# Output quarters eight slots behind instead of sixteen, reordered first loads and early attention, whole GpSimd masks, mx written over hp

## The chip, the cores and the metric

One core of a Trainium2 chip, one launch. The metric is the device time in microseconds (us). PE stands for TensorE's matmuls, PEld for its weight loads, DVE for VectorE, ACT for ScalarE, POOL for GpSimd. The profiler's span is some 1.7 us shorter than the time of the same execution (336.13 us timed, 334.4 us profiled, for the kernel before).

## The reference, cut to what matters

```python
# q, k, v: batch 8, heads 8, sequence 576, head size 64
scores = q @ k.T / 8
mask   = abs(pos_i - pos_j) <= 32            # sliding window
attn   = softmax(where(mask, scores, -1e9)) @ v
x      = attn as [4608 tokens, 512]
h      = x @ w_in                             # [4608, 2048]
g      = h if h >= 1; 0 if h <= -1; else (h + 1)**2 / 4
out    = g @ w_out                            # [4608, 512], float32
```

## The kernel before

The MLP is cut into 144 **slots**: 18 tiles of 256 tokens by 8 column chunks. Each slot runs 8 matmuls into `hp` and turns `hp` into a piece of `gT`. A slot's length is the time from its first hp matmul to that of the next slot, counted from the trace's records. Attention is woven in at fixed slots: `scores` (matmuls, Exp on ACT, then a multiplication by a 0/1 mask), `sums` (matmuls with `pt`, the masked exponentials, then the division, which gives `xT`), and transposes of q and k. The activation uses g = min(r, 1) * max(h, r) with r = relu(h/2 + 1/2).

```python
LAG = 16
for a in range(NF * NB + LAG):               # 144 slots + 16
    t, f = divmod(a, NF)
    eng = None if a < 14 else V if a < 28 else P       # who multiplies by the mask
    ...
        hp = ps_h.tile([128, 2, TB], FP, name="hp", tag="hp")     # PSUM, two buffers
        ... 8 matmuls xT, w_in -> hp ...
        rr = ewp.tile([128, 2, TB], FP, name="rr")                # SBUF
        A.activation(rr, hp, AF.Relu, scale=0.5, bias=0.5)
        mx = ewp.tile([128, 2, TB], FP, name="mx")                # SBUF
        V.tensor_max(mx, hp, rr)
        V.scalar_tensor_tensor(gT[t][...], rr, 1.0, mx, op0=ALU.min, op1=ALU.mult)
    ... attention events of this slot ...
    if a >= LAG:
        ... 4 matmuls gT, w_out -> op: the output of slot a - 16 ...

def mask(eng, p, m):
    if eng is P:                              # GpSimd: four pieces of 256 columns
        for h in range(2):
            for i in range(p.shape[2]):
                P.tensor_mul(p[:, h, i], p[:, h, i], m[:, h, i])
    elif eng is not None:
        eng.tensor_mul(p, p, m)
```

All loads of the start but the first q are issued by GpSimd in one sequence: most of w_in in pieces of 256 columns, then the rest of batch 0's q and k mixed with w_in, then batch 1, and w_out near the end.

The softmax here doesn't subtract the row's maximum and nothing guards it: scores larger than these inputs give would overflow.

## Time and profile before

| | before |
|---|---|
| time, median of the first 3 runs (range) | 337.27 us (335.68 to 337.89) |
| profiled span, granted TensorE clock | 334.4 us, 0.985 |
| PE busy | 310.2 us, 93% of the span |
| DVE, ACT, POOL busy | 236.2, 194.6, 160.9 us |
| PE idle up to 14.9 / to 52 / to 88 / to 315 / to the end | 1.2 / 10.4 / 2.9 / 5.7 / 4.0 us |

The last row is each stretch's length less its PE busy time, from the first table quoted in the prediction. The 93% hides what matters. Only 24 us of idle PE exist, 10 of them in one early stretch, and the last 15 us of busy PE are work that stands alone at the end only because it was postponed. With the PE's work unchanged, this kernel can get faster in two ways: less idle time of PE, or no PE work left over for a time when nothing else runs.

The view of waits of the kernel before (engine, line, what it waited for; us in total, number of times, longest), cut to the sums that wait for a GpSimd mask:

```profile
PE bb L294 <- POOL pt L201: 5.3, 7, 1.3
```

### The profile page before, as it was taken

What the parts mean: (1) busy time and instruction counts of PE and PEld (TensorE: products, weight loads), DVE (VectorE), ACT (ScalarE), POOL (GpSimd) and SP (SyncE); (2) the same over time, 40 slices, a digit from 0 to 9 for tenths busy, and PEclk for the clock granted to TensorE, in tenths of its full rate; (3) what the DMA queues carried; (4) which work ended last, traced back from release to release, by engine and by line L of the source; (5) the groups of instructions that cost most, each with busy time, mean ns of one, the idle gap of its engine ahead of it and who ended that gap; (6) DMA issues with size and microseconds to landing.
All of it is one profiled execution on the core that took longest, in us unless ns stands there. A gap on an engine that the chain in (4) does not pass through costs nothing.

```text
span 334.4 us, 8639 instructions
## 1 busy us (share of the span) xinstructions
PE 310.2 (93%) x3647; PEld 203.9 (61%) x3647; DVE 236.2 (71%) x355; ACT 194.6 (58%) x320; POOL 160.9 (48%) x236
## 2 busy tenths in 40 slices
PE   8957798979999989998999999997999999999995
PEld 3535575556666656665666666664666666666642
DVE  2343888778788777886788877885788877878800
ACT  3635894766765746565656656664675666544411
POOL 8986647950155973577524953297343334000000
PEclk9976999999999999999999999999999999999999
DMA  9999999999079997699440999179941100000021
GB/s 145 133 170 151 153 159 165 162 148 79 33 163 107 87 128 157 81 89 159 104 102 33 149 129 179 61 48 166 135 105 55 44 31 34 33 31 33 31 94 63
DMA packets 122118, 34.53 MB, mean 103 GB/s; under 512 B 108768, under 2 KB 117216, under 8 KB 122080
## 3 DMA queue, kind: packets, MB, share of 16 engines
q0 software_dynamic: 93216, 18.06, 71.1%
q1 hardware_dynamic: 28864, 15.93, 18.9%
q8 instruction: 28, 0.46, 0.6%
q14 instruction: 10, 0.08, 0.1%
HBM read 36.70 MB, written 9.44 MB: 138 GB/s over the span
## 4 chain that ended last, share of the span: by engine, by line
PE 53%; POOL 23%; issue 9%; ACT 6%; DVE 4%; DMA 3%; POOLq 0%; ACTq 0%
PE op L455 24%; PE hp L433 22%; POOL pt L201 10%; POOL vn L101 5%; PE bb L294 4%; POOL kn L93 3%; POOL qn L93 2%; ACT pt L236 2%; DMA kn<-in_k_dram 2%; DMA w_in<-in_moe_w_in_dram 2%; PE tp L184 1%; PE bb L228 1%; POOL w_in L105 1%; POOL kn L85 1%; DVE mx L439 1%
## 5 line engine op out<-in xcount | busy, mean ns | idle before, releaser
L433 PE MATMUL hp<-xT,w_in 128*128 128x256 bf16 x1152 | 151.0, 275 | 3.4 <-DVE xT L306 1.9
L455 PE MATMUL op<-w_out,gT 128*128 128x512 bf16 x576 | 145.6, 380 | 0.0
L433 PEld LDWEIGHTS <-w_in 128*128 128x128 bf16 x1152 | 111.9, 98 | 45.3 <-issue 4.7
L437 ACT ACTIVATE rr<-hp 128x512 f32<-128x512 f32 x144 | 85.8, 596 | 88.6 <-PE hp L433 82.5
L439 DVE TENSOR_TENSOR mx<-hp,rr 128x512 f32<-128x512 f32 x144 | 99.2, 689 | 37.7 <-ACT rr L437 36.7
L201 POOL TENSOR_TENSOR pt<-pt,mask 128x256 bf16<-128x256 bf16 (+1 forms) x112 | 72.2, 675 | 108.0 <-ACT pt L236 85.6
L440 DVE SCALAR_TENSOR_TENSOR gT<-rr,mx 128x512 bf16<-128x512 f32 x144 | 105.4, 732 | 4.9
L455 PEld LDWEIGHTS <-gT 128*128 128x128 bf16 x576 | 53.4, 98 | 42.8
L306 DVE TENSOR_TENSOR xT<-bb,rc 128x512 bf16<-128x512 f32 (+1 forms) x32 | 21.1, 658 | 29.4 <-ACT rc L301 29.4
L236 ACT ACTIVATE pt<-bb 128x1024 bf16<-128x1024 f32 (+1 forms) x33 | 33.2, 1011 | 12.8 <-PE bb L228 11.8
L459 ACT COPY osb<-op 128x512 f32<-128x512 f32 x36 | 21.0, 583 | 17.5 <-PE op L455 17.1
L294 PE MATMUL bb<-pt,ones 64*64 64x256 bf16 (+3 forms) x352 | 21.2, 256 | 9.2 <-POOL pt L201 5.3
L101 POOL DMA_DIRECT2D vn<-in_v_dram x32 | 27.7, 890 | 0.0
L301 ACT ACTIVATE rc<-lr 128x512 f32<-128x512 f32 (+2 forms) x40 | 23.5, 589 | 1.3
L294 PEld LDWEIGHTS <-ones 64*64 64x64 bf16 x352 | 11.7, 105 | 19.0 <-issue 15.6
L300 ACT ACTIVATE lr<-bb 128x512 f32<-128x512 f32 (+2 forms) x40 | 22.0, 550 | 0.7 <-PE bb L294 0.6
L294 PE MATMUL bb<-pt,vn 64*64 64x128 bf16 (+3 forms) x712 | 19.4, 204 | 0.0
L85 POOL DMA_DIRECT2D kn<-in_k_dram x24 | 13.0, 547 | 13.0 <-DMA w_out<-in_moe_w_out_dram 6.2
L294 PEld LDWEIGHTS <-vn 64*64 64x64 bf16 x712 | 17.0, 107 | 0.0
L228 PE MATMUL bb<-qT,kT 64*64 64x128 bf16 x520 | 13.5, 217 | 0.9 <-DVE kT L187 0.8
L93 POOL DMA_DIRECT2D qn<-in_q_dram x10 | 12.4, 1250 | 0.2 <-issue 0.2
L93 POOL DMA_DIRECT2D kn<-in_k_dram x10 | 12.3, 1238 | 0.0
(45 smaller groups left out, 105.9 us busy)
## 6 DMA issues: line engine op xcount, KB each, us to landing
out_dram<-osb SPq DMA_DIRECT2D x36, 256.0 KB, 2.1
vn<-in_v_dram POOLq DMA_DIRECT2D x32, 144.0 KB, 7.8
qn<-in_q_dram POOLq DMA_DIRECT2D x10, 288.0 KB, 6.2
kn<-in_k_dram POOLq DMA_DIRECT2D x10, 288.0 KB, 8.5
w_out<-in_moe_w_out_dram POOLq DMA_DIRECT2D x4, 512.0 KB, 8.5
kn<-in_k_dram POOLq DMA_DIRECT2D x24, 72.0 KB, 4.0
w_in<-in_moe_w_in_dram POOLq DMA_DIRECT2D x12, 128.0 KB, 5.0
qn<-in_q_dram POOLq DMA_DIRECT2D x20, 72.0 KB, 6.7
```

The costliest lines, as they stand in the source:

```text
L93: nc.gpsimd.dma_start(out=x[:, :, h], in_=src[b, NY * h:NY * h + NY].rearrange("y s d -> (y s) d") .rearrange("(u p) d -> p u d", p=128))
L101: nc.gpsimd.dma_start(out=vn[b][64 * a:64 * a + 64, :, h], in_=v[b, y:y + 2].rearrange("y s d -> (y s) d") .rearrange("(c r) d -> r c d", ...
L201: P.tensor_mul(p[:, h, i], p[:, h, i], m[:, h, i])
L236: A.activation(p, ps[:, :, :128 * n].rearrange(like, y=m), AF.Exp, scale=D ** -0.5)
L294: nc.tensor.matmul(bb[HD[h], a, o + c0:o + c1], ones[HD[a]] if c is None else vn[b][HD[a], c, h], p(a, h), start=n == 0, stop=True, skip_g ...
L300: A.activation(lr[:, :, :D0], bb[:, :, D0:2 * D0], AF.Ln)
L301: A.activation(rc[:, :, :D0], lr[:, :, :D0], AF.Exp, scale=-1.0)
L433: nc.tensor.matmul(hp[:, j], w_in[:, kk, 256 * f + 128 * j:256 * f + 128 * j + 128], xT[:, kk, r0:r0 + TB], start=n == 0, stop=n == 3)
L437: A.activation(rr, hp, AF.Relu, scale=0.5, bias=0.5)
L439: V.tensor_max(mx, hp, rr)
L440: V.scalar_tensor_tensor(gT[t][:, 2 * f:2 * f + 2], rr, 1.0, mx, op0=ALU.min, op1=ALU.mult)
L455: nc.tensor.matmul(op, gT[tt // 2][:, ff, 128 * (tt % 2):128 * (tt % 2) + 128], w_out[:, ff], start=ff == 0, stop=ff == 2 * NF - 1)
```

## The change

The intent: put part of the output matmuls into the waits of the start so that they don't stand at the end; bring what the start waits for sooner; shorten the GpSimd masks; and, with mx written over hp, take away the stretching of GpSimd's mask pieces and DVE's gT where they overlap (before, up to 1192 and 1148 ns, against medians of 668 and 692). The diff, cut to its core:

```diff
-    [w_in in eight pieces of 256 columns, then batch 0's rest mixed with w_in, then batch 1, v, w_out 0 to 3]
+    w = [(load_w_in, c, c + d, h) for c, d in ((0, 256), (256, 256), (512, 512), (1024, 512), (1536, 512)) for h in range(2)]
+    x = halves(0, 1)                                   # rest of batch 0's q (4 loads) and k (4)
+    put(w[:4] + x[:4] + w[4:5] + x[4:] + w[5:])
+    mix(halves(1, 0), [(load_w_out, 0)])
+    put([(load_w_out, 1), (load_w_out, 2)] + [(load_v, 1, n) for n in range(4)])
+    mix(halves(1, 1), [(load_w_out, 3)])
...
     def mask(eng, p, m):
-        if eng is P:
-            [four pieces]
-        elif eng is not None:
+        if eng is not None:
             eng.tensor_mul(p, p, m)
...
-    LAG = 16
+    PEM = 28
+    quarters = {11: ([], [0]), 12: ([], [1]), 13: ([], [2]), 14: ([], [4, 5]), 15: ([6], [3, 7])}
...
-    at(4, scores ...)  at(5, ...)  at(6, ...)  at(13, sums)  at(14, sums)
+    at(2, scores ...)  at(3, ...)  at(4, ...)  at(5, ...)  at(15, sums, sums)
-    for n, a in enumerate((12, 13, 20, 21, 22, 26, 27)):
+    for n, a in enumerate((11, 12, 19, 20, 22, 26, 27)):
         at(a, seq[n][1])
...
-    for a in range(NF * NB + LAG):
+    for a in range(NF * NB + NF):
...
-        eng = None if a < 14 else V if a < 28 else P
+        eng = None if a < 12 else V if a < PEM else P
+        pre, post = quarters.get(a, ([], [a - NF] if a >= 2 * NF else []))
...
-            mx = ewp.tile([128, 2, TB], FP, name="mx")
+            mx = ewp.tile([128, 2, TB], FP, name="mx") if a < PEM else hp
```

A **quarter** is four output matmuls. Four quarters make one 128-token output. Not shown in this cut: the transposes of the rest of batch 0's q and k move from slots 2 and 3 to slot 1, and two early slots instead of six take their hp from the output's PSUM buffers.

More of the change, by code (lines that the diff above doesn't have):

```diff
@@ L134 @@
         V.memset(t[:, 0:PAD], 0.0)
-    for c in range(0, 1024, 256):
-        for h in range(2):
-            load_w_in(c, c + 256, h)
     def mix(small, large):
@@ L146, in halves, with put @@
         return [(load_long, b, half, t, y) for t in range(2) for y in range(NY)]
-    mix(halves(0, 1), [(load_w_in, 1024, 1280, h) for h in range(2)] + [(load_w_in, 1280, 1536, h) for h in range(2)])
-    for h in range(2):
-        load_w_in(1536, 2048, h)
-    mix(halves(1, 0), [(load_v, 1, 0), (load_v, 1, 1)])
-    load_v(1, 2)
-    load_v(1, 3)
-    load_w_out(0)
-    load_w_out(1)
-    mix(halves(1, 1), [(load_w_out, 2)])
-    load_w_out(3)
+    def put(todo):
+        for fn, *x in todo:
+            fn(*x)
+    w = [(load_w_in, c, c + d, h) for c, d in ((0, 256), (256, 256), (512, 512), (1024, 512), (1536, 512)) for h in range(2)]
[4 more added lines that the diff above has]
+    mix(halves(1, 1), [(load_w_out, 3)])
     mix(halves(2, 0), [(load_v, 2, n) for n in range(4)])
-    for fn, *x in halves(2, 1):
-        fn(*x)
+    put(halves(2, 1))
     kT = {}
@@ L196, in mask @@
     def mask(eng, p, m):
-        if eng is P:
-            for h in range(2):
-                for i in range(p.shape[2]):
-                    P.tensor_mul(p[:, h, i], p[:, h, i], m[:, h, i])
-        elif eng is not None:
+        if eng is not None:
             eng.tensor_mul(p, p, m)
@@ L385, in steps @@
         yield (sums, b, 0, MAIN, S), (scores8, b)
-    at(4, (scores, 0, (0, 1), (0, 2), (2, 4)), (scores8, 0, ps_o))
-    at(5, (sums, 0, 0, TB, MAIN), (scores, 0, (1, 2), (0, 2), (2, 4)))
-    at(6, (sums, 0, 1, TB, MAIN, ps_s), (sums, 0, 0, MAIN, S))
+    at(2, (scores, 0, (0, 1), (0, 2), (2, 4)), (scores8, 0, ps_o))
+    at(3, (sums, 0, 0, TB, MAIN), (scores, 0, (1, 2), (0, 2), (2, 4)))
+    at(4, (sums, 0, 1, TB, MAIN, ps_s))
+    at(5, (sums, 0, 0, MAIN, S))
     seq = [x for b in range(1, B) for x in steps(b, 224)]
-    at(13, seq[0][0])
-    at(14, (*seq[1][0], ps_s))
-    for n, a in enumerate((21, 22, 23, 27)):
+    at(15, seq[0][0], (*seq[1][0], ps_s))
+    for n, a in enumerate((20, 22, 23, 27)):
         at(a, seq[2 + n][0])
-    for n, a in enumerate((12, 13, 20, 21, 22, 26, 27)):
+    for n, a in enumerate((11, 12, 19, 20, 22, 26, 27)):
         at(a, seq[n][1])
@@ L400 @@
         at(a, seq[6 + n][0], seq[7 + n][1] if n < len(sl) - 1 else None)
-    for b, half, *a in ((0, 1, 2, 3), (1, 0, 9, 11), (1, 1, 18, 19), (2, 0, 24, 25), (2, 1, 28, 29)):
+    for b, half, *a in ((0, 1, 1, 1.5), (1, 0, 9, 10), (1, 1, 17, 18), (2, 0, 24, 25), (2, 1, 28, 29)):
         for t in range(2):
@@ L410, with quarter @@
             xps.setdefault(a + 9 + 2 * t, []).append((b, t))
-    gT = {}
-    for a in range(NF * NB + LAG):
+    gT, op = {}, {}
+    def quarter(x):
+        tt, ff = divmod(x, 4)
+        if tt not in op:
+            op[tt] = ps_o.tile([128, DM], FP, name="op", tag="op"), []
+        o, done = op[tt]
+        for j in range(4 * ff, 4 * ff + 4):
+            nc.tensor.matmul(o, gT[tt // 2][:, j, 128 * (tt % 2):128 * (tt % 2) + 128], w_out[:, j],
+                             start=not done, stop=len(done) == 2 * NF - 1, skip_group_check=True)
+            done.append(j)
+        if len(done) == 2 * NF:
+            osb = osp.tile([128, DM], FP, name="osb")
+            A.copy(osb, o)
+            nc.sync.dma_start(out=out[128 * tt:128 * tt + 128, :], in_=osb)
+    for a in range(NF * NB + NF):
         t, f = divmod(a, NF)
-        eng = None if a < 14 else V if a < 28 else P
+        eng = None if a < 12 else V if a < PEM else P
+        pre, post = quarters.get(a, ([], [a - NF] if a >= 2 * NF else []))
         for b, x in loads.get(a, []):
@@ L426 @@
             r0 = TB * t % RING
-            if a < LAG and a % 4 > 1 and not 3 < a < 8:
+            if a in (6, 7):
                 hp = ps_o.tile([128, 2, TB], FP, name="hp", tag="op")
@@ L437 @@
             A.activation(rr, hp, AF.Relu, scale=0.5, bias=0.5)
-            mx = ewp.tile([128, 2, TB], FP, name="mx")
+            mx = ewp.tile([128, 2, TB], FP, name="mx") if a < PEM else hp
             V.tensor_max(mx, hp, rr)
             V.scalar_tensor_tensor(gT[t][:, 2 * f:2 * f + 2], rr, 1.0, mx, op0=ALU.min, op1=ALU.mult)
+        for x in pre:
+            quarter(x)
         ends = []
@@ L449 @@
             end()
-        if a >= LAG:
-            for x in range(4 * (a - LAG), 4 * (a - LAG) + 4):
-                tt, ff = divmod(x, 2 * NF)
-                if ff == 0:
-                    op = ps_o.tile([128, DM], FP, name="op", tag="op")
-                nc.tensor.matmul(op, gT[tt // 2][:, ff, 128 * (tt % 2):128 * (tt % 2) + 128], w_out[:, ff],
-                                 start=ff == 0, stop=ff == 2 * NF - 1)
-                if ff == 2 * NF - 1:
-                    osb = osp.tile([128, DM], FP, name="osb")
-                    A.copy(osb, op)
-                    nc.sync.dma_start(out=out[128 * tt:128 * tt + 128, :], in_=osb)
-        if a in tps:
-            copies = [tpose(b, n, t, (A.copy, V.tensor_copy)[i if a > LAG else 0], tp1((ps_s, ps_n)[i]))
-                      for i, (b, n, t) in enumerate(tps[a])]
+        for x in post:
+            quarter(x)
+        for part in (a, a + 0.5):
+            copies = [tpose(b, n, t, (A.copy, V.tensor_copy)[i if a > 15 else 0], tp1((ps_s, ps_n)[i]))
+                      for i, (b, n, t) in enumerate(tps.get(part, []))]
             for x in copies:
```

## The prediction

> **What bounds the kernel now.** I read the busy time of each engine by stretch first, because shares of the whole span mix stages. The columns after the stretch are its length, then busy us of PE, PEld, DVE, ACT and POOL, the granted TensorE clock, and the DMA's share and rate.
>
> ```profile
> 0.00:14.90 14.90, 13.71 (x168) 6.88 (x169) 4.26 (x18) 8.17 (x11) 13.16 (x28) 1.00 1.26 138
> 14.90:52.00 37.10, 26.66 (x427) 19.64 (x426) 23.32 (x37) 23.59 (x40) 25.82 (x43) 0.86 1.22 160
> 52.00:88.00 36.00, 33.11 (x457) 21.79 (x457) 28.56 (x45) 22.68 (x36) 16.84 (x23) 1.00 1.56 126
> 88.00:315.00 227.00, 221.35 (x2527) 148.63 (x2526) 177.62 (x256) 136.63 (x228) 105.11 (x144) 1.00 0.79 91
> 315.00:334.40 19.40, 15.36 (x75) 7.01 (x72) 2.44 (x4) 3.53 (x6) 0.00 (x0) 1.00 0.18 68
> ```
>
> Up to 52 us the PE waits for loads and for the first attention batch: 10.4 us idle, at a mean clock of 0.86. From 88 to 315 us the PE is the bound (5.7 us idle). From 315 us on only the PE works. The PE's timeline shows the tail, and the pace of a slot (one pass of the main loop: 8 hp matmuls, and from slot 16 on 4 op matmuls):
>
> ```profile
> 312.91 1.04 PE L433 MATMUL hp<-xT,w_in 128*128 128x256 bf16 x8
> 313.79 1.03 PE L455 MATMUL op<-w_out,gT 128*128 128x512 bf16 x4
> 314.65 1.04 PE L433 MATMUL hp<-xT,w_in 128*128 128x256 bf16 x8
> 315.52 14.84 PE L455 MATMUL op<-w_out,gT 128*128 128x512 bf16 x68
> ```
>
> Starts differ by 0.87 us, so a slot without attention costs 1.74 us of PE, and four op matmuls 0.87. The last line is the price of a lag of 16 slots: 64 of these 68 matmuls were owed from the start, when w_out had not come.
>
> The start, in the same view:
>
> ```profile
> 21.81 1.17 PE L184 MATMUL tp<-ident,qn 128*64 128x128 bf16 x18 [3.17 <-DMA qn<-in_q_dram]
> 27.14 1.17 PE L184 MATMUL tp<-ident,kn 128*64 128x128 bf16 x18 [2.34 <-DMA kn<-in_k_dram]
> 38.46 1.91 PE L433 MATMUL hp<-xT,w_in 128*128 128x256 bf16 x16 [1.08 <-DVE xT L309]
> 52.09 0.82 PE L433 MATMUL hp<-xT,w_in 128*128 128x256 bf16 x6 [1.48 <-DVE xT L306]
> ```
>
> The rest of batch 0's q and k, queued behind and between w_in, stops PE twice; the last line is inside slot 16, which so starts in effect at about 51.7 us (52.09 less two matmuls already done).
>
> In the steady stretch four slots (45, 62, 81, 99) are longer than their matmuls need, by 1.7, 1.7, 0.7 and 2.4 us as PE's matmul starts show: 6.5 us, all in front of sums that wait for a GpSimd mask. The POOL timeline before the last of them:
>
> ```profile
> 217.82 2.69 POOL L201 TENSOR_TENSOR pt<-pt,mask 128x256 bf16<-128x256 bf16 x4 [6.43 <-ACT pt L236]
> 220.46 2.50 POOL L93 DMA_DIRECT2D qn<-in_q_dram  x2
> 222.95 2.44 POOL L93 DMA_DIRECT2D kn<-in_k_dram  x2
> 225.35 3.44 POOL L101 DMA_DIRECT2D vn<-in_v_dram  x4
> 228.73 3.56 POOL L201 TENSOR_TENSOR pt<-pt,mask 128x256 bf16<-128x256 bf16 x4
> ```
>
> Mask, loads and mask form one chain of 14.5 us on POOL. The second mask takes 3.56 us where others take 2.5, and the two lines' own views (ns min/median/max) say why:
>
> ```profile
> L201 POOL TENSOR_TENSOR pt<-pt,mask x112: 361/668/1192, 91.0 to 284.2; 128x256 bf16<-128x256 bf16 x88, 128x96 bf16<-128x96 bf16 x24
> L440 DVE SCALAR_TENSOR_TENSOR gT<-rr,mx x144: 691/692/1148, 17.7 to 317.1; 128x512 bf16<-128x512 f32 x144
> ```
>
> Both have a tail of about 1.15 us, and in the timeline these long ones overlap each other.
>
> [...] gT (rr and mx, both SBUF) stretches from 692 to 1148 ns, while mx (one PSUM input) never exceeds 693. [...] In this trace undisturbed starts are 0.625 us apart at 256 columns and 0.32 at 96, so 1.9 ns per column and 0.14 us fixed[...]. [...] matmuls between 20.3 and 30.5 us start 213 ns apart instead of 108, after PE stood from 18.6 to 21.8.
>
> **Part by part.**
>
> *Tail.* The output runs 8 slots behind instead of 16. Eight quarters of four op matmuls move ahead of slot 16: 8 x 0.87 = **-6.9 us** at the end, where nothing lies beside them. Total PE work is unchanged, so this is gained only if the early stretch takes these 6.9 us in its waits: the question is when slot 16 starts.
>
> *Loads and early stretch.* In the before trace POOL's issues wait for the transfer eight issues earlier, which dates landings: the first w_in piece at 14.3 us, the eighth at 19.1, so 896 KB in 4.8 us or 186 KB/us. The new order is 512 KB w_in, 288 qn, 256 w_in, 288 kn, 256 w_in, then 1024 w_in. At that rate qn lands at 17.7 us (21.8 before), kn at 20.6 (27.1), the third w_in piece near 22. Pure w_in of 512 columns ran slower (110 KB/us of written bytes by my count of the trace's packets around 24.5 us), so I place the end of w_in at 29 to 30 us, the next q and k at 34 to 35.5, and, scaling the mean of 151 KB/us that the old order kept to 52 us, w_out 1 and 2 at 38 and 41, v of batch 1 at 45, w_out 3 at 47.5.
> PE from slot 2 (about 22.5): I add slot by slot the matmul work that the old trace shows (hp 0.87, 18 transposes 0.72, scores with their mask 0.9, two sums 1.3, quarter 0.87): slots 2-5 6.5, 6-8 2.6, 9-10 3.2, 11-14 9.4, 15 4.7: 26.4 us. The clock should be halved in part again (PE idles from 17 to 22 here too): +2.3 us of it. Slot 16 would come at 51.2, but needs xT from the sums in slot 15; before, xT came 3 us after such sums, which makes 52 to 53. Against 51.7: **+1 us**. So I expect no earlier slot 16, only eight quarters done for free in the old waits.
>
> *Masks 20 to 30.* Scores are a slot further ahead of their sums in the one place (slot 22) where sums waited 1.3 us for a DVE mask: **-1.2 us**.
>
> *Whole GpSimd masks, mx in PSUM.* One mask of 1024 columns: 0.14 + 1024 x 1.9 ns = 2.1 us, against 2.5 undisturbed. With mx written over hp, gT has one SBUF input, so the extra 1.0 us of a disturbed mask goes too. In the chain above the first mask gives 0.5 and the second 1.4 us back, of a wait of 2.4; the other three waits (1.7, 1.7, 0.7) are below such a gain and vanish. **-6.0 us** (6.5 less 0.5 left).
>
> *Price of mx in PSUM.* hp is now freed by gT, 0.73 us later. In plain slots of the old trace gT ends 0.35 us (0.30 at the end) before the next hp into that buffer starts, so nothing stalls. In 17 slots it ends later than, or within 60 ns of, that start, 3.8 us in sum; without the stretched gT about 1.3 us remains: **+1.3 us**.
>
> Sum: 337.3 - 6.9 + 1.0 - 1.2 - 6.0 + 1.3 = 325.5 us.
>
> **Rivals.** (a) *The start takes the tail's gain.* If w_in in 64-partition pieces keeps 110 KB/us, or the halved clock lasts to 30.5 us, slot 16 slips 2 to 4 us: 328 to 330. For: the 10 us at half clock, and PE has 6.9 us more to do before slot 16. Against: qn and kn come 4 and 6 us sooner. (b) *hp's release becomes the bound.* If a PSUM destination, or reading and writing one bank at once, makes mx or gT over 0.3 us longer, each of 116 slots stalls: 0.1 us beyond the slack is 12 us, giving 337 or worse. Against: PSUM sources cost nothing visible (xT and mx 692 ns, like gT); an in-place PSUM write occurs nowhere in this trace. (c) *The start gains too.* If DMA keeps 186 KB/us and the clock stays up, slot 16 starts 3 to 4 us sooner: 321. (d) *A whole mask is not cheaper*, or its four-dimensional pattern is slow: then 2 to 4 us of POOL waits stay: 328.
>
> **Range and chances.** The tail is nearly sure, masks likely; start and hp release carry the spread. 320 to 332 holds (a), (c) and (d) one at a time. Faster by over 2% is below 330.5: it needs only the tail and no large loss: 0.83. Within 2%: 0.15, mostly (a) with (d), or a mild (b). Slower: 0.02.
>
> **What would show it.** The closing run of op matmuls is 36 long and about 7.8 us. Slot 16's hp starts between 50 and 54 us with eight quarters ahead of it. qn's transposes start near 18 us, kn's near 21. Masks on POOL take 2.1 us in one piece, gT's maximum falls to about 0.7, and sums in slots 45, 62 and 81 wait for no POOL. Some hp matmuls wait 0.1 to 0.5 us for gT. Wrong if plain slots grow past 1.74 us, if mx exceeds 0.8 us, or if slot 16 starts after 55 us.

## The result, and the profile after

| | before | after |
|---|---|---|
| median of 4 runs (range) | 337.39 us (335.68 to 337.89) | 325.55 us (325.25 to 326.03) |
| ratio of fast runs (95% interval) | | 0.9664 (0.9635 to 0.9693) |
| profiled span, clock | 334.4 us, 0.985 | 323.9 us, 0.994 |
| PE idle in the five stretches | 1.2 / 10.4 / 2.9 / 5.7 / 4.0 us | 1.3 / 7.3 / 2.3 / 1.8 / 4.0 us |

A ratio is the mean time of one kernel's fast runs over that of the other's of the same rounds, so not quite the ratio of the medians.

The busy time by stretch of the kernel after (length, then busy us of PE, PEld, DVE, ACT and POOL, granted clock, DMA share and rate). The fourth stretch ends at 304.5 so that the last is as long as before (19.4 us):

```profile
0.00:14.90 14.90, 13.57 (x169) 6.80 (x170) 4.34 (x18) 8.17 (x11) 13.25 (x28) 1.00 1.26 143
14.90:52.00 37.10, 29.81 (x448) 20.96 (x446) 23.99 (x37) 22.20 (x38) 21.40 (x36) 0.95 1.20 162
52.00:88.00 36.00, 33.67 (x445) 21.58 (x443) 27.47 (x42) 24.75 (x40) 18.58 (x26) 1.00 1.53 137
88.00:304.50 216.50, 214.74 (x2498) 143.60 (x2498) 168.42 (x250) 134.10 (x223) 85.45 (x60) 1.00 0.81 94
304.50:323.90 19.40, 15.45 (x91) 8.61 (x89) 8.04 (x12) 5.33 (x9) 0.00 (x0) 0.98 0.14 54
```

In the second stretch PE is 3.2 us busier, and in the fourth it idles 1.8 us instead of 5.7. In the last stretch DVE has 8.0 us of work where it had 2.4: the slots now reach further into it.

The PE timeline of the kernel after: start, and the tail's line.

```profile
18.16 0.69 PE L179 MATMUL tp<-ident,qn 128*64 128x128 bf16 x18 [1.08 <-DMA qn<-in_q_dram]
21.88 0.69 PE L179 MATMUL tp<-ident,kn 128*64 128x128 bf16 x18 [3.02 <-DMA kn<-in_k_dram]
23.16 1.86 PE L442 MATMUL hp<-xT,w_in 128*128 128x256 bf16 x8 [0.59 <-DMA w_in<-in_moe_w_in_dram]
...
34.75 1.91 PE L442 MATMUL hp<-xT,w_in 128*128 128x256 bf16 x16 [1.32 <-DVE xT L299]
...
38.00 1.03 PE L442 MATMUL hp<-xT,w_in 128*128 128x256 bf16 x8 [0.72 <-DVE mx L448]
...
54.28 0.81 PE L442 MATMUL hp<-xT,w_in 128*128 128x256 bf16 x6 [0.69 <-DVE xT L296]
...
312.02 7.93 PE L413 MATMUL op<-w_out,gT 128*128 128x512 bf16 x36
```

The q and k transposes come 3.7 and 5.3 us sooner than before. Yet the matmuls that follow slot 16's wait for xT start 2.2 us later (54.28 against 52.09), with eight quarters done by then. The tail is 36 output matmuls instead of 68, and 6.9 us shorter.

The POOL timeline of the kernel after, before slot 99:

```profile
215.21 2.13 POOL L193 TENSOR_TENSOR pt<-pt,mask 128x1024 bf16<-128x1024 bf16 x1 [7.30 <-ACT pt L226]
217.28 2.50 POOL L93 DMA_DIRECT2D qn<-in_q_dram  x2
219.76 2.44 POOL L93 DMA_DIRECT2D kn<-in_k_dram  x2
222.16 3.44 POOL L101 DMA_DIRECT2D vn<-in_v_dram  x4
225.55 2.20 POOL L193 TENSOR_TENSOR pt<-pt,mask 128x1024 bf16<-128x1024 bf16 x1
```

The chain is 12.5 us long instead of 14.5. The masks and DVE's two lines of the kernel after in the view of lines (ns min/median/max):

```profile
L193 POOL TENSOR_TENSOR pt<-pt,mask x28: 913/2127/2209, 92.0 to 279.2; 128x1024 bf16<-128x1024 bf16 x22, 128x384 bf16<-128x384 bf16 x6
L448 DVE TENSOR_TENSOR hp<-hp,rr x116: 689/700/700, 86.0 to 312.9; 128x512 f32<-128x512 f32 x116
L449 DVE SCALAR_TENSOR_TENSOR gT<-rr,hp x116: 686/687/689, 86.8 to 313.6; 128x512 bf16<-128x512 f32 x116
```

No mask is stretched (at most 2209 ns, median 2127), and gT's tail of 1148 ns is gone (at most 689). The price is in the waits of the kernel after: the long waits for masks have gone from the list's head, and a short one, 18 times, has come in, namely w_in's weight load into an hp that gT has not yet freed.

```profile
PEld L442 <- DVE gT L449: 6.4, 18, 0.8
```

That figure is PEld's idle time, not PE's. From PE's matmul starts I count 1.6 us of delay in nine slots.

### Where the time went, in the profiled pair

| term | predicted | measured | how measured |
|---|---|---|---|
| slot 16 resumes | +1.0 | +2.2 | 52.09 to 54.28 |
| from there to slot 30 | -1.2 | -1.2 | 35.59 to 34.37; slot 22 went from 3.73 to 2.50 |
| slots 30 to 142 | -6.0 + 1.3 = -4.7 | -4.5 | 227.0 to 222.5 |
| tail | -6.9 | -6.9 | 14.84 to 7.93 |
| sum | -11.8 | -10.4 | spans: -10.5 |

The slots that had waited for masks, 45, 62, 81 and 99, went from 4.36, 4.36, 3.35 and 5.08 us to 2.55, 2.56, 2.56 and 3.35. The hp waits added 1.6 us elsewhere. Slots 30 to 142 are what is called the steady stretch below: from slot 30's first hp matmul to slot 143's. It is the most repeatable part: 222.5 us in the changed kernel, when it was run again, and in e4 to e8, whatever the start was.

### The profile page after: what moved, and what is told of

The parts are those of the page before. It is cut to its first block, busy times and chain, and to the rows that moved or that the text cites.

```text
span 323.9 us, 8547 instructions
## 1 busy us (share of the span) xinstructions
PE 307.2 (95%) x3643; PEld 201.5 (62%) x3643; DVE 232.3 (72%) x356; ACT 194.6 (60%) x320; POOL 138.7 (43%) x148
## 4 chain that ended last, share of the span: by engine, by line
PE 70%; POOL 8%; ACT 7%; DVE 7%; issue 5%; DMA 2%; ACTq 0%; POOLq 0%
PE op L413 31%; PE hp L442 31%; PE bb L284 5%; DVE gT L449 2%; PE bb L218 2%; POOL vn L101 2%; DMA w_in<-in_moe_w_in_dram 2%; ACT pt L226 2%; DVE mx L448 1%; ACT rr L446 1%; ACT lr L290 1%; POOL pt L193 1%; DVE hp L448 1%; POOL kn L85 1%; ACT osb L418 1%
## 5 line engine op out<-in xcount | busy, mean ns | idle before, releaser
L193 POOL TENSOR_TENSOR pt<-pt,mask 128x1024 bf16<-128x1024 bf16 (+1 forms) x28 | 52.6, 1877 | 122.5 <-ACT pt L226 96.4
L448 DVE TENSOR_TENSOR hp<-hp,rr 128x512 f32<-128x512 f32 x116 | 81.0, 698 | 26.1 <-ACT rr L446 24.6
L449 DVE SCALAR_TENSOR_TENSOR gT<-rr,hp 128x512 bf16<-128x512 f32 x116 | 79.7, 687 | 4.0
L448 DVE TENSOR_TENSOR mx<-hp,rr 128x512 f32<-128x512 f32 x28 | 19.3, 688 | 17.3 <-ACT rr L446 17.3
L284 PE MATMUL bb<-pt,ones 64*64 64x256 bf16 (+3 forms) x352 | 19.5, 255 | 2.3 <-POOL pt L193 0.7
L449 DVE SCALAR_TENSOR_TENSOR gT<-rr,mx 128x512 bf16<-128x512 f32 x28 | 19.4, 692 | 1.0
L284 PE MATMUL bb<-pt,vn 64*64 64x128 bf16 (+3 forms) x712 | 18.2, 204 | 0.0
L85 POOL DMA_DIRECT2D kn<-in_k_dram x24 | 13.1, 554 | 10.7 <-issue 3.3
L284 PEld LDWEIGHTS <-ones 64*64 64x64 bf16 x352 | 10.6, 105 | 11.1 <-issue 7.8
```

The lines of the kernel that those rows point to most:

```text
L284: nc.tensor.matmul(bb[HD[h], a, o + c0:o + c1], ones[HD[a]] if c is None else vn[b][HD[a], c, h], p(a, h), start=n == 0, stop=True, skip_g ...
L449: V.scalar_tensor_tensor(gT[t][:, 2 * f:2 * f + 2], rr, 1.0, mx, op0=ALU.min, op1=ALU.mult)
```

## The experiments

Four runs of each kernel, beside the kernel before on the same chip. Three chips were used, with four experiments on each: e1 to e4, e5 to e8, and the repeated changed kernel with e9 to e11. The changed kernel itself ran beside e9 to e11 only, so "over the changed kernel" means, for e1 to e8, over its runs of the result. The ratios to before have intervals 1 to 2% wide, and differences of 1 us between experiments are read from the slots of the profiles, not from them.

**Theory:** the gain is the tail (-6.9) and the steady stretch (-4.5), and the start, though it has eight quarters more to do, loses little because they lie in old waits and because the loads come sooner. **Rivals:** whole masks alone would do what masks and in-place mx do together; quarters are worth little (or all) of the tail; the gain of the start is one of clock only.

### e1: whole masks, mx in SBUF as before

```diff
-            mx = ewp.tile([128, 2, TB], FP, name="mx") if a < PEM else hp
+            mx = ewp.tile([128, 2, TB], FP, name="mx")
```

> The changed kernel, but mx is a tile of SBUF in every slot, as before; whole GpSimd masks stay. Theory [...]: gT's maximum goes back to over 1.0 us, masks that meet it grow from 2.1 to about 3 us, and some 2 us more of PE waiting for masks returns in slots 45, 62 and 99, while the 1.6 us of hp matmuls that wait for gT vanish. Sum about +0.5 us against the changed kernel, ratio to before about 0.968. Rival (hp's later release is the larger cost, contention is small): faster than the changed kernel by 1.6 us, ratio 0.961 to 0.962.

Measured: 326.29 us (325.94 to 327.85), ratio 0.9743 (0.9673 to 0.9813), span 324.4, 0.5 over the changed kernel's. The size was as expected, the mechanism not. The masks hardly stretched (median 2172, at most 2387 ns). In their place gT was stretched, up to 2596 ns. A mask in e1's POOL timeline, the gT beside it in its DVE timeline, gT's line, and a matmul of slot 48 that waited in e1's PE timeline:

```profile
118.31 2.19 POOL L193 TENSOR_TENSOR pt<-pt,mask 128x1024 bf16<-128x1024 bf16 x1
```

```profile
118.46 2.60 DVE L449 SCALAR_TENSOR_TENSOR gT<-rr,mx 128x512 bf16<-128x512 f32 x1
```

```profile
L449 DVE SCALAR_TENSOR_TENSOR gT<-rr,mx x144: 691/692/2596, 17.7 to 314.1; 128x512 bf16<-128x512 f32 x144
```

```profile
126.34 1.03 PE L442 MATMUL hp<-xT,w_in 128*128 128x256 bf16 x8 [0.56 <-DVE mx L448]
```

gT began 0.15 us after the mask's start and ended 0.56 us after its end: as gT takes 0.69 us alone, some 0.13 us of it (an estimate from these figures) had been done when the mask was over. The reverse shows too, in the same timelines: a mask that began at 110.18 with 0.33 us of a gT left took 2.32 us, one that began at 122.49, when no gT ran, 2.11. The hp waits of the changed kernel are gone, and slots 45, 62 and 99 are 0.26, 0.25 and 0.13 us longer. Slots 47 and 64 are longer by 0.73 each, because the next slot's hp waits for an mx that stood behind such a gT. The steady stretch took 222.9 us.

### e2: masks in four pieces, mx over hp

```diff
     def mask(eng, p, m):
-        if eng is not None:
+        if eng is P:
+            for h in range(2):
+                for i in range(p.shape[2]):
+                    P.tensor_mul(p[:, h, i], p[:, h, i], m[:, h, i])
+        elif eng is not None:
             eng.tensor_mul(p, p, m)
```

> The changed kernel, but each GpSimd mask in four pieces again, mx stays in PSUM. Theory: four pieces cost 2.5 us undisturbed against 2.1, and are no longer stretched by gT; slot 99 waits some 0.8 us more, the other three stay without a wait or nearly: +0.5 to +1.0 us against the changed kernel, ratio about 0.969. Rival (the whole masks, not mx, took the waits away): +4 us or more, ratio 0.978.

Measured: 327.97 us (326.41 to 329.91), ratio 0.9783 (0.9714 to 0.9851), span 325.5 (+1.6, where 0.5 to 1.0 was expected). The pieces take at most 766 ns, where they reached 1192 in the kernel before, so it is with mx in SBUF, as gT's second SBUF input, that they stretch (e3, which differs from e2 in this alone, has 1222). Slots 45, 62, 81 and 99 take 3.04, 2.98, 2.55 and 3.99 us, and the steady stretch 224.0.

### e3: both undone

Edit: e1's and e2's together.

> The changed kernel with both undone: four-piece masks and mx in SBUF, so only the loads, the early events and the lag of 8 are left of the change. Theory: the waits of slots 45, 62, 81 and 99 return (5.7 us) and the hp waits for gT go (1.6 us): +4.1 us against the changed kernel, ratio about 0.978 to 0.979. Rival (the waits would not return, because the shifted schedule moved them): within 1 us of the changed kernel.

Measured: 331.16 us (330.44 to 331.57), ratio 0.9872 (0.9816 to 0.9929), span 328.6 (+4.7). Slots 45, 62, 81 and 99 are back at 4.36, 4.35, 3.35 and 5.08 us, the figures of the kernel before, and the steady stretch at 227.0, the same as before. Both lines of e3:

```profile
L195 POOL TENSOR_TENSOR pt<-pt,mask x112: 360/668/1222, 92.3 to 285.4; 128x256 bf16<-128x256 bf16 x88, 128x96 bf16<-128x96 bf16 x24
L453 DVE SCALAR_TENSOR_TENSOR gT<-rr,mx x144: 691/692/1143, 17.8 to 318.4; 128x512 bf16<-128x512 f32 x144
```

With short pieces both stretch, to 1222 and 1143 ns; with a whole mask (e1) gT reaches 2596 ns and the mask 2387 at most, of a median of 2172.

From the steady stretch of these three and the changed kernel: whole masks alone -4.1 us (e1), in-place mx alone -2.9 (e2: -4.6 of mask waits, +1.6 of hp waits), both -4.5. The two cures treat the same waits, so they don't add.

### e4: the kernel before, with only these two

```diff
-        if eng is P:
-            [four pieces]
-        elif eng is not None:
+        if eng is not None:
             eng.tensor_mul(p, p, m)
...
-            mx = ewp.tile([128, 2, TB], FP, name="mx")
+            mx = ewp.tile([128, 2, TB], FP, name="mx") if a < 28 else hp
```

> The kernel before with whole GpSimd masks and mx written over hp from slot 28 on, nothing else. Theory: it gains what the part is worth alone, 4.1 us, ratio about 0.988, with gT never over 0.70 us and hp waits of 0.2 to 0.4 us after late slots. Rival (the part only pays together with the new start): within 1 us of before.

Measured: 330.12 us (329.17 to 331.56), ratio 0.9848 (0.9787 to 0.9908). The kernel before had 335.21 on this chip (its slowest run, 339.0, was slow and is left out of the ratio), so -5.1 us. Slots 45, 62, 81 and 99 take 2.55, 2.57, 2.55 and 3.35 us, and the steady stretch 222.5, as in the changed kernel. The gain does not depend on the rest of the change.

### e5: no quarters ahead, lag 16, everything else as changed

```diff
-    quarters = {11: ([], [0]), 12: ([], [1]), 13: ([], [2]), 14: ([], [4, 5]), 15: ([6], [3, 7])}
+    quarters = {}
...
-    for a in range(NF * NB + NF):
+    for a in range(NF * NB + 2 * NF):
...
-        pre, post = quarters.get(a, ([], [a - NF] if a >= 2 * NF else []))
+        pre, post = quarters.get(a, ([], [a - 2 * NF] if a >= 2 * NF else []))
```

> The changed kernel, but with no early quarters: output runs 16 slots behind again; loads, early events and masks as changed. Theory (quarters before slot 16 are only partly free, because PE is busy without a gap from 38 to 54 us in the changed kernel): slot 16's xT wait then ends when batch 1's v lets the sums run, near 50 us against 54.3, and the closing run is 68 op matmuls, 14.7 us against 7.8: +6.9 - 4.3 = +2.6 us against the changed kernel, profiled span about 326.5. Rival (my prediction's wording: the eight quarters are free, taken from waits): slot 16 stays at 54 us, +6.9 us, span about 331.

Measured: 331.93 us (328.58 to 332.32), ratio 0.985 (0.9784 to 0.9915), span 330.3, +6.4. The PE timeline of e5 around slot 16, and its tail (one matmul record is missing there):

```profile
47.41 1.03 PE L442 MATMUL hp<-xT,w_in 128*128 128x256 bf16 x8 [0.90 <-DVE mx L448]
...
51.32 0.38 PE L442 MATMUL hp<-xT,w_in 128*128 128x256 bf16 x2 [2.03 <-DVE xT L296]
52.06 1.44 PE L442 MATMUL hp<-xT,w_in 128*128 128x256 bf16 x6 [0.36 <-DVE xT L296]
55.00 1.25 PE L442 MATMUL hp<-xT,w_in 128*128 128x256 bf16 x8
...
311.44 14.84 PE L413 MATMUL op<-w_out,gT 128*128 128x512 bf16 x67
```

From the start of slot 11 to the resumption in slot 16, e5 takes 11.2 us (40.89 to 52.06) and the changed kernel 14.7 (39.59 to 54.28). Eight quarters are 6.95 us of PE. So half of them (3.4) lies in waits for DVE (mx in slots 14 and 15, xT before slot 16), and half (3.5) is added to the path. Without them the PE stands idle in those waits, and the clock is then halved from 52.0 to 55.4 us (0.57 in the mean from 52.06 to 56.00; the six matmuls at 52.06 take 1.44 us instead of 0.81), which costs 1.6 us (from the resumption to slot 17's start 2.94 us and slot 17 2.67, against 1.52 and 2.46 in the changed kernel). The account of +6.4: tail +6.9, slots 11 to 16 -3.5, a start that was 1.3 later in e5's profile (its mean clock of 0.982 leaves, by estimate, some 7 us of halved clock before 39.6, where the changed kernel has 3.41), halved clock +1.6; together +6.3. Three of the four runs had a clock of 0.982 or 0.983. The one at 0.993 took 328.58 us, which fits the expected +2.6 (+3.0 over the changed kernel's median); the other three lie 6.3 to 6.8 over it. In number that is near the rival's +6.9, but not in mechanism, for the rival had slot 16 stay at 54 us and the trace has it at 52.06 after a later start.

### e6: the old order of the loads

```diff
-    put(w[:4] + x[:4] + w[4:5] + x[4:] + w[5:])
-    mix(halves(1, 0), [(load_w_out, 0)])
-    put([(load_w_out, 1), (load_w_out, 2)] + [(load_v, 1, n) for n in range(4)])
-    mix(halves(1, 1), [(load_w_out, 3)])
+    [the sequence of the kernel before]
```

> The changed kernel, but the transfers in the order and sizes of before; early events, quarters and masks as changed. Theory: q's transposes wait until about 21.8 us and k's until 25 to 27, slot 2 starts at 26 to 28 instead of 23.2 and runs at half clock for longer, and w_out 3 lands near 52: slot 16's xT wait ends at 57 to 59, +3 to +5 us against the changed kernel, span 327 to 329. Rival (the order of loads does not matter, since the DMA queues are busy in either): within 1 us.

Measured: 330.24 us (328.67 to 331.5), ratio 0.9819 (0.9764 to 0.9874), span 328.2, +4.3, as expected. Two lines of e6's PE timeline, whose partners after stand at 21.88 and 54.28:

```profile
26.84 1.17 PE L188 MATMUL tp<-ident,kn 128*64 128x128 bf16 x18 [3.21 <-DMA kn<-in_k_dram]
...
58.56 0.82 PE L451 MATMUL hp<-xT,w_in 128*128 128x256 bf16 x6 [0.68 <-DVE xT L305]
```

k comes 5.0 us later, slot 2 4.8 and slot 16 4.3, and that is the whole difference: from slot 16's resumption on the two kernels take the same time to 0.02 us. The new order is worth a little more than the quarters cost at the start (3.5, e5). Without it the lag of 8 would have slipped the start by 6.5 us against before.

### e7: ten warm matmuls while PE waits for k

```diff
             for x in copies:
                 x()
+            if part == 1:
+                keep_warm(10, ps_h, "hp")
```

> The changed kernel with 10 more matmuls on zeros between the q and the k transposes of slot 1, where PE waits 3 us for kn. Theory [...]: the halved window goes, slot 2 takes 1.9 us instead of 3.1, and all of the DVE-bound stretch after it comes 1.0 to 1.2 us sooner: span about 322.8, and a mean clock of 1.00 up to the end. Rival (the start is set by ACT, DVE or transfers, so the clock costs nothing): span within 0.3 us of 323.9.

Measured: 324.49 us (324.24 to 326.39), ratio 0.9663 (0.9611 to 0.9714), span 322.6, -1.3. In the changed kernel the clock was halved (0.50) from 22.74 to 26.15 us, and 0.87 in the mean from 14.9 to 28.2; in e7 it was 1.00 over that stretch. So slot 2 runs at full clock in e7's PE timeline:

```profile
17.84 2.12 PE L318 MATMUL z<-warm 128*128 128x512 bf16 x9
...
23.07 1.03 PE L442 MATMUL hp<-xT,w_in 128*128 128x256 bf16 x8 [0.59 <-DMA w_in<-in_moe_w_in_dram]
```

These eight matmuls took 1.86 us in the changed kernel. So the halved clock cost the changed kernel 1.3 us by the profiled pair, not the 2.3 that the prediction had put in. (The medians differ by 1.1 us, on different chips, and one of e7's runs, at 326.39, was slower than all four of the changed kernel's.)

### e8: batch 1's first sums one slot sooner

```diff
-    at(15, seq[0][0], (*seq[1][0], ps_s))
+    at(14, seq[0][0], (*seq[1][0], ps_s))
```

> The changed kernel with batch 1's first two sums in slot 14 instead of 15. Theory: batch 1's v has landed by 47 us, so the sums run on time, and slot 16's hp no longer waits 0.85 us for xT: -0.8 us, span about 323.1. Rival (v lands later than that): PE waits for v in slot 14 and the span is the same or longer.

Measured: 324.68 us (324.15 to 325.29), ratio 0.9657 (0.9602 to 0.9711), span 322.9, -1.0. Slot 16's eight hp matmuls run from 53.08 without a wait, where the changed kernel waited 0.85 us for xT. v had come in time.

### The changed kernel again

No edit; on the third chip.

> The changed kernel as it is, once more, on the chip of these runs, as the measure for the three beside it. Expected 325.2 to 326.2 us with a span of 323.5 to 324.3 and one half-clock window of 3.4 us; the kernel before spreads over 333 to 339 us as in the earlier runs, so the ratio may lie anywhere from 0.965 to 0.975.

Measured: 325.75 us (324.78 to 326.5), ratio 0.9733 (0.9688 to 0.9777), span 324.2. The kernel before had 334.38 here (333.46 to 336.74). See the next chapter.

### e9: warm matmuls, sums in slot 14, and v loaded three slots later

```diff
-            loads.setdefault(a + t, []).append((b, t))
+            loads.setdefault(a + (0, 1, 5)[t], []).append((b, t))
```

and the edits of e7 and e8. v's four issues then come after the mask they stood in front of.

> The changed kernel with the warm matmuls of slot 1, batch 1's sums in slot 14, and the later batches' v issued three slots later, so that on POOL the second mask comes before v's 3.4 us of issues. Theory: the gains add where they are independent: 1.3 (clock), 0.8 to 1.0 (sums), 0.8 (slot 99's wait for its mask goes, as the mask no longer stands behind v): span 320.6 to 321.2, time about 322.6. Rival (v of batch 1 lands too late once everything before it is quicker): 0.5 to 1 us of the sums' gain is lost, span about 321.8.

Measured: 324.27 us (323.22 to 325.18), ratio 0.9692 (0.9651 to 0.9732), profiled span 323.4, the other runs' 321.4, 321.9 and 323.1. Slot 99's last wait is gone (2.55 us). In the profiled run, which was the slowest, the third w_in piece came late: PE waited 2.83 us for it at 24.41, and the eight matmuls that followed took 1.86 us, as at the halved clock of the changed kernel, where e7's took 1.03. So e9's edits worked where the trace shows them, and in this run the late piece took the gain back: slot 11 began 2.4 us later than in e7. The median missed the expected 322.6 us by 1.7. Why the three unprofiled runs missed it too isn't shown.

### e10: e9 with batch 1's second transposes a slot sooner

```diff
-    for b, half, *a in ((0, 1, 1, 1.5), (1, 0, 9, 10), (1, 1, 17, 18), (2, 0, 24, 25), (2, 1, 28, 29)):
+    for b, half, *a in ((0, 1, 1, 1.5), (1, 0, 9, 10), (1, 1, 16, 17), (2, 0, 24, 25), (2, 1, 28, 29)):
```

> The run beside it, and batch 1's second half of transposes in slots 16 and 17 instead of 17 and 18. Theory: the scores of slot 19 no longer wait 0.55 us for kT's copy: 0.5 us less than the run beside it, span 320.1 to 320.7. Rival (q of that half lands after slot 16, or its copies delay slot 16's mx): the same or longer.

Measured: 323.82 us (323.43 to 324.58), ratio 0.9682 (0.9646 to 0.9717), span 321.7. Against e9, slot 19 went from 2.71 to 2.19 us, but slot 20 from 2.80 to 3.31, for its sums now waited 0.60 us for DVE's mask: the wait had only moved. From slot 16's resumption to slot 30 e10 takes 34.38 us and e9 34.37, so the edit gained nothing there. This is still the best version found, 1.9 us below the changed kernel on the same chip (ranges 323.43 to 324.58 and 324.78 to 326.5 do not meet) and faster than both; its runs can't be told from e9's (323.22 to 325.18).

### e11: the kernel before, kept warm at the start

```diff
+        if a in (2, 3):
+            keep_warm(12, ps_h, "hp")
         if a in tps:
```

> The kernel before with 12 matmuls on zeros in slots 2 and 3, where PE waits for qn and kn. Theory (half clock for one to three windows is part of the slow and uneven start of before): the halved windows mostly go, slots 3 and 4 take 1 to 2 us less together, the span falls from 331 to 335 by 1 to 2 us, and its runs spread less than 2 us. Rival (the uneven start is the transfers' alone): mean and spread of its runs as before's.

Measured: 335.64 us (333.88 to 337.08), ratio 1.003 (0.9982 to 1.0079): the same. Two stretches of e11 (columns as above):

```profile
14.90:28.00 13.10, 11.41 (x99) 6.84 (x98) 6.07 (x9) 4.39 (x8) 11.37 (x20) 1.00 1.13 148
230.00:233.50 3.50, 2.71 (x33) 1.65 (x34) 0.00 (x0) 2.00 (x4) 1.34 (x3) 0.51 3.00 139
```

The clock was full at the start (1.00), and the 10.2 us of halved clock that the kernel before has there (0.50 from 20.32 to 30.56) were gone, without a gain in time that can be measured (the interval leaves room for 0.2%, 0.6 us). So the higher mean clock of the changed kernel (0.994 against 0.985) is not where its gain came from: in the kernel before, the halved clock lay beside waits for transfers (3.17 us for q before 21.81, 2.34 for k before 27.14). Two of e11's runs had a clock of 1.000 throughout and took 333.88 and 335.64 us, inside the 333.46 to 336.74 of before. Yet among the 21 runs of the kernel before on the three chips, those at a clock of 0.979 took 336.7 to 339.0 us (the slowest is the slow run) and those at 0.993 to 0.995 took 333.5 to 335.0: clock and time go together there, and only the experiment shows that a better clock alone does not bring the time. One qualification: in this profile slot 16 resumed at 50.23, 1.9 us sooner than in the profile of before, but e4, with the same start as before and halved clock, had 50.5; so it was an early draw, or a small gain that was lost again when the clock was halved after slot 99's mask wait (second line). These runs cannot part the two.

## Why the prediction was right, and where it was not

**Tail: right.** -6.9 us, 36 matmuls in 7.93 us.

**Loads: nearly right in the landings.** q's transposes came at 18.16 and k's at 21.88, where 18 and 21 were forecast. e6 shows that slot 16 follows the loads: k 5.0 us later, slot 16 4.3.

**Start: the term "+1 us" was mis-sized, measured +2.2.** Its result, slot 16 between 50 and 54 us, held (53.21), but the sum behind it had wrong terms. Slot 2 began at 23.16, not at 22.5. From slot 2 to slot 16 it had 26.4 us of matmuls and 2.3 of halved clock, 28.7; the trace shows 30.05. The halved clock was 1.3 (e7). And 2.4 us of waits were left out: 1.5 in slot 7, for xT, and 0.9 in slot 9, for mx. The busy time of one more stretch of the kernel after (columns as above) shows why:

```profile
28.20:39.60 11.40, 9.09 (x157) 7.33 (x149) 10.22 (x17) 8.82 (x16) 7.82 (x11) 1.00 1.03 163
```

DVE is busy 10.2 of 11.4 us and PE 9.1: in that stretch DVE sets the pace. (This is read from the trace; no run took work from DVE there.) The prediction counted PE's work there and no other engine's. "Eight quarters done for free in the old waits" was thus half right: e5 shows 3.4 of 6.95 us hidden, 3.5 paid, and the new order of the loads paying for it (e6). They also kept the clock from falling after slot 16 (1.00 from 52 to 60 us, where e5, without them, has 0.57 from 52.06 to 56.00), which nobody had counted. And the +2.2 hangs on one profile of before: e4, with the same start as before, resumed slot 16 at 50.54 instead of 52.09, against which the changed kernel is 3.7 later.

**Slots 16 to 30: right**, -1.2 us, in slot 22 as named.

**Whole masks and in-place mx: the sum was right, the split between the two was not.** Predicted -6.0; the four slots give 6.1 (17.15 to 11.02 us in sum; 0.8 of wait is left in slot 99, so there were 6.9 and not the 6.5 that the prediction read), and a mask takes 2.13 us where 2.1 was forecast. But the prediction gave the end of the stretching to the in-place mx alone. e1 shows that a whole mask hardly stretches (2.39 us at most) even with gT's two SBUF inputs: in the timelines read there the one that started first kept its time (a mask 2.19 us, a gT 0.69) and the other was stretched (gT to 2.60 us, a mask to 2.32). That mx in place would end the stretching was the estimate from the trace of before, where mx, with one PSUM input, never exceeded 693 ns, beside masks either; e2 bears it out (766 ns at most). The in-place mx adds only 0.4 us to whole masks in the steady stretch (222.9 to 222.5), because the hp waits take back 1.6 of the 2.1 that it gives.

**Price of hp's later release: right.** +1.3 predicted, +1.6 counted, and gone in e1.

**Rivals.** (a) did not happen as told: slot 16 slipped 1.2 us beyond the forecast, not 2 to 4, and by DVE, not by w_in, for which PE waited 0.59 us. (b) fell: an in-place max takes 700 ns instead of 692, gT with mx in PSUM 687 instead of 692, and plain slots stayed at 1.74 us. (c) was not seen in the changed kernel. (d) fell: 2127 ns, and no slot's mask wait stayed but slot 99's 0.8 us.

**What was luck.** The absolute time was right to 0.1 us, and it is steady (325.55 and 325.75 on two chips). The difference is less so. The kernel before had medians of 337.39, 335.21, 335.65 and 334.38 us in four groups of runs, since its start hangs on when transfers land (with the same loads, k's transposes began at 27.14 us before, at 25.41 in e4 and at 26.75 in e11); the profiled pair differs by 10.4 us, not 11.8, as the profiled run of before, 336.13, lay below its median. The start that was 1.2 us worse than forecast was made good by that. On the third chip the change is worth 8.6 us between medians. So it is worth 9 to 12 us, and which of these a group of runs shows depends on the kernel before.

**Left open:** what decides when a transfer lands from run to run (e9's profile lost some 2.4 us to one late piece of w_in and the halved clock beside it), what the earlier attention events are worth alone, whether keeping the kernel before warm has a small gain, and how idle PE must be for the clock to fall. Before the fall at 22.74 in the changed kernel PE had been busy for 0.69 of 3.44 us, before the one near 52.0 in e5 for 1.06 of 3.41, and before the one near 230.1 in e11 for 1.74 of 3.41; in the kernel before it was busy for 1.76 of the 3.41 us up to 231.93, in slot 99 as in e11, and the clock stayed at 1.00.

## What to carry to other kernels

Postponed work of the bounding engine costs its full length at the end, where nothing lies beside it (here 6.9 us); moved into an early stretch with waits it costs only what the waits don't cover, but count every engine's work of that stretch and not the bounding engine's alone, since here DVE was the busiest for 11 us. Two cures for one conflict did not add here (-4.1 and -2.9 us alone, -4.5 together): run each alone before crediting either. And before taking a halved clock for a loss, ask whether the engine was waiting for a transfer anyway: the warm-up matmuls gained 1.3 us, by the profiles, where PE was what the rest waited for, and nothing that could be measured where it was not.
